# Finished PSUM banks through ScalarE and accumulating transfers instead of VectorE adds: a fused attention and MLP block on one core

## The chip, the cores and the metric

The kernel runs on one core of one Trainium2 chip. The metric is the time of one execution on the device in microseconds; the median of several runs is given. One further execution was profiled, and its trace is what the views quoted here are taken from. The engines are called TensorE (PE), VectorE (DVE), ScalarE (ACT), GpSimd (POOL) and SyncE (SP, which here only issues transfers).

## What is computed

One input `x` of 2048 rows by 576 columns, in float32, is normalised by row. The output is the sum of three things: `x` itself, a sliding local dilated attention of the normalised rows, and a two-layer MLP with a ReLU of the normalised rows.

```python
xn = _layernorm(x, axis=-1)
return x + _A_ref(xn, A_wqkv, A_wo) + _B_ref(xn, B_w1, B_w2)

# _A_ref: 32 heads of 18, each row attends to 8 rows: itself and 2, 4, .. 14 rows before
qkv = x @ wqkv
logits = einsum("bhsd,bhswd->bhsw", q, kg) * scale      # then masked, softmax over the 8
o = einsum("bhsw,bhswd->bhsd", attn, vg)
return o @ wo                                           # 576 x 576
# _B_ref: 576 -> 4608 -> 576
h = maximum(x @ w1, 0)
return h @ w2
```

## The kernel before

**Two phases, row tiles and slots.** The 2048 rows are split in two phases (`ph`) of 1024 rows: the even rows and the odd rows, so that the dilation of two stays within a phase. A phase has eight row tiles of 128 rows (`i`), which the MLP takes in pairs as four row blocks of 256 (`tb`). The 4608 hidden columns are 36 blocks of 128 (`f`), taken three at a time: `C = 3` blocks make a chunk (`c`), and a phase has `NCH = 12` chunks. The list `slots` runs over phase, chunk, row block and hidden block, in this order: 2 x 12 x 4 x 3 = 288 slots. One slot computes one hidden block for one row block (`h_two`, two slots at once and two slots ahead, on the two halves of the rows of TensorE's array) and multiplies an earlier one with its part of `w2` (`o_two`, or `o_mm` in the first seven and the last three slots).

**Precision.** Every operand of a matmul is held as a high and a low part, which a copy on ScalarE (L170, L651) and a subtraction on VectorE (L174, L654) make; each product is three matmuls.

**The output sums.** The three slots of one chunk and row block form a group. They add up in four PSUM banks, `PO[k, h]`: `k` is the row tile of the pair, `h` the half of the columns (`CUT`: 256 and 320). At the last slot of a group (`f == C - 1`) `o_out` empties the four banks: VectorE adds each to the tile `X[ph, i]`, which was loaded with the input rows and so gathers the residual, the MLP and, in chunk `WO_CHUNK = 10`, the output projection of the attention, whose matmuls go to the same banks. In the last chunk the tile is stored by SP one slot later. The next group's matmuls use the same four banks again, after the `h_two` of their first slot.

**Order of the work.** The order on each engine is written out by hand; nothing reorders it. `at(n, ...)` and `late(n, ...)` put a step into slot n, ahead of or behind its `o_two`; `run_splits(n)` at the beginning of a slot splits the weights that are due and has SP load the next staging tile `st`; `run_bg(margin(n))` at the end hands VectorE pieces of the attention as long as its planned time `t["dve"]` stays within `margin` of TensorE's `t["pe"]`. Each `o_out` advances `t["dve"]` for its four adds. Units of attention begin at slot 10 of a phase and every 24 slots after; each has eight slots in which `qkv_tile` adds its matmuls. GpSimd has little to do: memsets for k and v, a mask (`affine_select`), copies of parts of q, and the inverse deviations of the normalisation.

**Buffers.** `xp` has 11 buffers for the tiles `X`: eight of a phase and three more, which `wo_turn` uses for turned tiles of the attention's output before the next phase's rows are loaded into them.

Of the kernel before, what the change touches and what calls it, by code (L numbers as in the profile page):

```python
# [10 lines left out]
F32 = mybir.dt.float32  # L11
F32R = mybir.dt.float32r
AF = mybir.ActivationFunctionType
ALU = mybir.AluOpType
# [4 lines left out]
P = 128  # L19
NPH = 2  # L20
NI = 8
NTB = 4
# [4 lines left out]
C = 3  # L27
# [16 lines left out]
FIRST = 4  # L44
# [14 lines left out]
def tile_body(ctx: ExitStack, tc: tile.TileContext, x, wqkv, wo, w1, w2, out):  # L59
    nc = tc.nc  # L60
    S, D = x.shape
# [4 lines left out]
    NCH = NF // C  # L66
# [3 lines left out]
    CUT = (slice(0, 256), slice(256, D))  # L70
# [6 lines left out]
    pool = lambda name, bufs, **k: ctx.enter_context(tc.tile_pool(name=name, bufs=bufs, **k))  # L77
# [5 lines left out]
        pool(name, 1).tile([P, words], F32, name=name)  # L83

    consts = pool("consts", 1)
    xp = pool("xp", 11)
    xtp = pool("xtp", NTB)
    qop = pool("qop", 1)
    kp = pool("kp", 1)
# [31 lines left out]
    o_v = out.rearrange("(p i two) d -> two i p d", i=NI, two=NPH)  # L121


    t = {"pe": 0.0, "dve": 0.0}
# [16 lines left out]
    def dve(n):  # L141
        t["dve"] += (n + 70) / 960.0
# [113 lines left out]
    X, XT, XN, MR = {}, {}, {}, {}  # L256
# [307 lines left out]
    def run_bg(margin):  # L564

        ran = False
        while bg and t["dve"] + bg[0][0] / 960.0 <= t["pe"] + margin and not (ran and bg[0][0] == 0):
            n, f, a = bg.popleft()
            f(*a)
            if n:  # L570
                ran = True
                dve(n)
# [55 lines left out]
    slots = [(ph, c, tb, f) for ph in range(NPH) for c in range(NCH) for tb in range(NTB) for f in range(C)]  # L628
    H, PO = {}, {}
# [64 lines left out]
    def o_two(n):  # L694


        ph, c, tb, f = slots[n]
        hi, lo = H.pop(n)
        w = W2[ph, c, f]
        with_wo = c == WO_CHUNK and f == C - 1  # L700
        if f == 0:
            o_tiles(n)

        def run(k, h, upper):
            cs, first = slice(k * P, (k + 1) * P), k == upper
            z = [(l[:, cs], w[:, b, W2CUT[h]]) for l, b in ((hi, 0), (hi, 1), (lo, 0))]
            if with_wo:
                more = wo_run(ph, 2 * tb + k, h, (UPPER_MORE if upper else LOWER_MORE) if first else (UPPER if upper else LOWER), upper)
                z = z + more
            return [  # L710
                (PO[k, h], l, r, f == 0 and first and j == 0, f == C - 1 and not first and j == len(z) - 1, CUT[h].stop - CUT[h].start)
                for j, (l, r) in enumerate(z)
            ]

        for j in range(4):
            k, h = divmod(j, 2)
            behind = PB[j - 2] if j > 1 else PB[3] if j == 0 and f else None
            PB[j] = mm_rows((run(k, h, False), run(1 - k, h, True)), behind)
        if with_wo:
            for k in range(2):  # L720
                OT.pop((ph, 2 * tb + k))
        o_out(n, rows=True)
# [3 lines left out]
    def o_mm(n, out=True, which=range(2)):  # L726
        ph, c, tb, f = slots[n]
        hi, lo = H[n]
        w = W2[ph, c, f]
        end = n == len(slots) - 1  # L730
        if f == 0 and 0 in which:
            o_tiles(n)
        for k in which:
            cs = slice(k * P, (k + 1) * P)
            terms = [(j, l, b, h) for j, (l, b) in enumerate(((hi, 0), (hi, 1), (lo, 0))) for h in range(2)]
            if end:
                terms.sort(key=lambda z: -z[3])
            for j, l, b, h in terms:
                mm(
                    PO[k, h], l[:, cs], w[:, b, W2CUT[h]],  # L740
                    f == 0 and j == 0, f == C - 1 and j == 2, D2,
                )
        if 1 in which:
            H.pop(n)
        if out:
            o_out(n, which)

    def store(ph, i):
        nc.sync.dma_start(o_v[ph, i], X[ph, i])

    def o_out(n, which=range(2), rows=False):
        ph, c, tb, f = slots[n]
        if f < C - 1:
            return
        end = n == len(slots) - 1
        t["dve"] = max(t["dve"], t["pe"] - 0.4)
        order = [(k, h) for k in which for h in range(2)]
        if rows:
            order.sort(key=lambda z: z[1])
        elif end:  # L760
            order.sort(key=lambda z: (z[0], -z[1]))
        for k, h in order:
            i = 2 * tb + k
            acc, cols = X[ph, i], CUT[h]
            nc.vector.tensor_tensor(acc[:, cols], PO[k, h], acc[:, cols], op=ALU.add)  # L765
            dve(cols.stop - cols.start)
            if end and k:
                (nc.scalar if h else nc.sync).dma_start(o_v[ph, i][:, cols], acc[:, cols])
            elif end and h == 0:
                store(ph, i)  # L770
            elif c == NCH - 1 and h == 1 and not end:
                at(n + 1, store, ph, i)


    todo = {}

    def at(n, f, *a):
        todo.setdefault(n, []).append((f, a))
# [3 lines left out]
    def late(n, f, *a):  # L782
        todo_late.setdefault(n, []).append((f, a))
# [61 lines left out]
    both, x_low, w_low, last = TERMS[0:4], TERMS[4:8], TERMS[9:13], [TERMS[8], TERMS[13]]  # L845
# [61 lines left out]
    h4[0]()  # L907
    h4[1]()
    o_out(2, (0,))
    x4 = make_xt(0, 4, parts=True)  # L910
    for f in x4[:3]:
# [11 lines left out]
        (late if k else at)(z, {"stats": stats, "norm": norm, "xt": make_xt}[op], 0, *a)  # L923
    for tb in range(NTB):
        late((8, 8, 9, 7)[tb], twin, tb)
    def margin(n):

        odd, qkv = n % 2 == 0, n + 1 in qkv_slots
        if n + 1 in busy_m | bounded and not qkv:
            return 1.4  # L930
        due = sum(z[0] <= n + 1 for z in (*staged, *tasks))
        if slots[n][3] == 1:
            return (1.8 if odd else 2.7 + 2.4 * qkv) - 0.8 * due + 1.6 * (odd and qkv)
        return (2.5 if odd else 3.5 + 2.4 * qkv) - 0.8 * due + 1.6 * (odd and qkv)
# [6 lines left out]
    for n in range(FIRST, len(slots)):  # L941
        if n == ROW0:
            AHEAD["n"] = 4
        run_splits(n)
        g = n - n % 2 + LAG
        if n < ROW0:
            h_mm(n + LAG)
        elif g < len(slots):
            h_two(g, n % 2 == 1)
        for f, a in todo.pop(n, []):  # L950
            f(*a)
        if ROW0 - 1 <= n < len(slots) - C:
            o_two(n)
        else:
            o_mm(n)
        for f, a in todo_late.pop(n, []):
            f(*a)
        run_bg(margin(n))
# [27 lines left out]
```

## Time and profile before

| | |
|---|---|
| median of 3 runs | 1143.41 us (1143.14 to 1143.69) |
| span of the profiled execution, first to last instruction | 1141.6 us |
| TensorE busy | 1134.5 us, 99% |
| VectorE busy | 802.1 us, 70% |
| ScalarE busy | 303.0 us, 27% |
| GpSimd busy | 57.1 us, 5% |
| moved by the DMA engines | 83.6 MB, 73 GB/s |

The profile gives no other time for the profiled execution than its span; the median of the runs is 1.8 us above it. The page has the busy time of each engine, the span in 40 slices, the DMA queues, the chain of work that ended last, groups of instructions by line with what they waited for, and DMA issues. A line such as L765 is a line of the kernel; where a helper issues the instruction it is the helper's line. Busy time on TensorE is modelled from the ends of pipelined matmuls.

### The profile page before, as it was taken

What the parts mean: (1) busy time and instruction counts of PE and PEld (TensorE: products, weight loads), DVE (VectorE), ACT (ScalarE), POOL (GpSimd) and SP (SyncE); (2) the same over time, 40 slices, a digit from 0 to 9 for tenths busy, and PEclk for the clock granted to TensorE, in tenths of its full rate; (3) what the DMA queues carried; (4) which work ended last, traced back from release to release, by engine and by line L of the source; (5) the groups of instructions that cost most, each with busy time, mean ns of one, the idle gap of its engine ahead of it and who ended that gap; (6) DMA issues with size and microseconds to landing.
All of it is one profiled execution on the core that took longest, in us unless ns stands there. A gap on an engine that the chain in (4) does not pass through costs nothing.

```text
span 1141.6 us, 38695 instructions
## 1 busy us (share of the span) xinstructions
PE 1134.5 (99%) x17224; PEld 1128.4 (99%) x17224; DVE 802.1 (70%) x1522; ACT 303.0 (27%) x854; POOL 57.1 (5%) x84
## 2 busy tenths in 40 slices
PE   8999999999999999999999999999999999999998
PEld 8999999999999999999999999999999999999998
DVE  7415886887788689854674179868868887896433
ACT  4412222222232212322462122222222312222110
POOL 2400000000000000000110000000000000010000
PEclk9999999999999999999999999999999999999999
DMA  6303212130330312622633033032221304136002
GB/s 192 109 2 94 71 47 67 48 98 6 97 98 13 104 33 50 175 57 63 157 122 98 2 101 88 23 85 63 63 59 47 107 2 114 45 81 152 13 2 84
DMA packets 118855, 83.60 MB, mean 73 GB/s; under 512 B 33201, under 2 KB 102449, under 8 KB 118689
## 3 DMA queue, kind: packets, MB, share of 16 engines
q1 hardware_dynamic: 118256, 80.67, 25.6%
q8 instruction: 135, 2.21, 0.8%
q10 hardware_dynamic: 432, 0.46, 0.1%
q14 instruction: 32, 0.25, 0.1%
HBM read 64.95 MB, written 7.96 MB: 64 GB/s over the span
## 4 chain that ended last, share of the span: by engine, by line
PE 96%; issue 2%; DVE 1%; ACT 0%; DMA 0%; DVEq 0%; POOL 0%; ACTq 0%
PE po L137 41%; PE pm L137 28%; PE ph L137 24%; PE ph L127 1%; PE po L127 1%; PE pm L317 0%; DVE pr L544 0%; DMA x<-in_x 0%; PE pm L369 0%; DVE xn L613 0%; PE pm L127 0%; DVE hlo L654 0%; DVE x L765 0%; ACT xT L322 0%; DVE xn L614 0%
## 5 line engine op out<-in xcount | busy, mean ns | idle before, releaser
L137 PE MATMUL po<-w2t,hhi 64*128 64x256 f32 (+1 forms) x4448 | 444.8, 290 | 0.0
L137 PEld LDWEIGHTS po<-w2t,hhi 64*128 64x128 f32 x4448 | 356.1, 184 | 0.6
L137 PE MATMUL po<-w2t,hlo 64*128 64x256 f32 (+1 forms) x2224 | 331.2, 287 | 0.0
L137 PE MATMUL ph<-xT,w1t 64*128 64x256 f32 x4806 | 305.5, 273 | 0.3 <-DVE hlo L654 0.2
L137 PEld LDWEIGHTS ph<-xT,w1t 64*128 64x128 f32 x4806 | 293.7, 184 | 1.5 <-DVE hlo L654 1.1
L765 DVE TENSOR_TENSOR x<-po,x 128x320 f32<-128x320 f32 (+1 forms) x384 | 149.6, 449 | 149.4 <-PE po L137 146.8
L137 PEld LDWEIGHTS po<-w2t,hlo 64*128 64x128 f32 x2224 | 217.2, 184 | 0.0
L651 ACT ACTIVATE hhi<-ph 128x256 fp32r<-128x256 f32 x187 | 62.1, 382 | 496.8 <-PE ph L137 484.6
L137 PE MATMUL pm<-wq,xT 64*128 64x432 f32 x1728 | 178.8, 354 | 0.0
L137 PE MATMUL pm<-xT,w1t 64*128 64x256 f32 x2700 | 170.6, 273 | 0.0
L137 PEld LDWEIGHTS pm<-xT,w1t 64*128 64x128 f32 x2700 | 164.5, 184 | 0.0
L137 PEld LDWEIGHTS pm<-wq,xT 64*128 64x128 f32 x1728 | 160.0, 184 | 2.9
L654 DVE SCALAR_TENSOR_TENSOR hlo<-ph,hhi 128x256 fp32r<-128x256 f32 x187 | 70.8, 418 | 129.6 <-ACT hhi L651 129.5
L651 ACT ACTIVATE hhi<-pm 128x256 fp32r<-128x256 f32 x101 | 33.3, 381 | 214.1 <-PE pm L137 214.1
L505 DVE TENSOR_TENSOR pr<-qo,k 128x1152 f32<-128x1152 f32 x64 | 85.6, 1348 | 0.0
L508 DVE TENSOR_REDUCE lg<-pr 128x64 f32<-128x1152 f32 x64 | 85.3, 1342 | 0.0
L537 DVE TENSOR_TENSOR pr<-lg,v 128x1152 f32<-128x1152 f32 x64 | 85.0, 1348 | 0.3
L544 DVE TENSOR_TENSOR pr<-pr 128x288 f32<-128x288 f32 (+1 forms) x128 | 70.1, 600 | 0.1
L654 DVE SCALAR_TENSOR_TENSOR hlo<-pm,hhi 128x256 fp32r<-128x256 f32 x101 | 38.2, 418 | 32.9 <-ACT hhi L651 32.1
L170 ACT ACTIVATE w2t<-st 128x256 fp32r<-128x256 f32 (+1 forms) x144 | 56.3, 445 | 7.1 <-PE po L137 3.9
L174 DVE TENSOR_TENSOR w2t<-st,w2t 128x256 fp32r<-128x256 f32 (+1 forms) x142 | 57.9, 448 | 0.1
L174 DVE TENSOR_TENSOR w1t<-st,w1t 128x640 fp32r<-128x640 f32 x68 | 55.6, 817 | 2.4 <-ACT w1t L170 2.2
(99 smaller groups left out, 689.8 us busy)
## 6 DMA issues: line engine op xcount, KB each, us to landing
st<-in_w SPq DMA_DIRECT2D x72, 288.0 KB, 3.3
st<-in_w SPq DMA_DIRECT2D x72, 256.0 KB, 3.1
st<-in_wqkv SPq DMA_DIRECT2D x32, 216.0 KB, 3.0
st<-in_w SPq DMA_DIRECT2D x144, 32.0 KB, 2.8
out<-x SPq DMA_DIRECT2D x15, 288.0 KB, 2.4
x<-in_x SPq DMA_DIRECT2D x14, 288.0 KB, 4.4
k<-k SPq DMA_DIRECT2D x8, 441.0 KB, 3.9
v<-v SPq DMA_DIRECT2D x8, 441.0 KB, 4.7
```

What stands on the lines that cost most here:

```text
L127: nc.tensor.matmul(o, l, r, start=start, stop=stop)
L137: ins = nc.tensor.matmul(o, l[z], r[z], start=start, stop=stop)
L170: nc.scalar.activation(hi, src, AF.Copy)
L174: nc.vector.tensor_tensor(lo, src, f32(hi), op=ALU.subtract)
L505: nc.vector.tensor_tensor(pr[i], q, window(k, i), op=ALU.mult)
L508: nc.vector.tensor_reduce(lg[:, i], pr.pop(i).rearrange(heads, d=Dh), axis=AX.X, op=ALU.add)
L537: nc.vector.tensor_tensor(pr[i].rearrange(heads, d=Dh), e, window(v, i).rearrange(heads, d=Dh), op=ALU.mult)
L544: nc.vector.tensor_tensor(o, z[:, 0:n], z[:, n : 2 * n], op=ALU.add)
L651: nc.scalar.activation(hi, pt, AF.Relu)
L654: nc.vector.scalar_tensor_tensor(lo, pt, 0.0, f32(hi), op0=ALU.max, op1=ALU.subtract)
L765: nc.vector.tensor_tensor(acc[:, cols], PO[k, h], acc[:, cols], op=ALU.add)
```

## The change

The output sums are no longer kept in the chip's memory through the phase. Chunk 0 of a phase still adds the banks to `X` on VectorE, but writes the result to a staging tile `ev`, which SP stores to the output. In each later chunk ScalarE copies the four banks to two staging tiles, and when both halves of a tile are there, GpSimd issues a transfer that adds the tile to the output in memory (`accum_op`). The pool `evp` has three staging tiles, which take the room of the three buffers by which `xp` becomes smaller. The very last group is handled in another way: `last_sums`, in slot 285, has SP load the two output tiles back to staging tiles, VectorE adds the last banks to them, and they are stored. There are 174 accumulating transfers of 128 x 576 words (288 KB). The planned time of VectorE no longer counts the adds that are gone.

```diff
-    xp = pool("xp", 11)
+    xp = pool("xp", 8)
+    evp = pool("evp", 3)
...
-    def store(ph, i):
-        nc.sync.dma_start(o_v[ph, i], X[ph, i])
-
     def o_out(n, which=range(2), rows=False):
...
         end = n == len(slots) - 1
-        t["dve"] = max(t["dve"], t["pe"] - 0.4)
+        last = ph == NPH - 1 and c == NCH - 1 and tb == NTB - 1
+        if c == 0 or last:
+            t["dve"] = max(t["dve"], t["pe"] - 0.4)
...
         for k, h in order:
             i = 2 * tb + k
-            acc, cols = X[ph, i], CUT[h]
-            nc.vector.tensor_tensor(acc[:, cols], PO[k, h], acc[:, cols], op=ALU.add)
-            dve(cols.stop - cols.start)
-            if end and k:
-                (nc.scalar if h else nc.sync).dma_start(o_v[ph, i][:, cols], acc[:, cols])
-            elif end and h == 0:
-                store(ph, i)
-            elif c == NCH - 1 and h == 1 and not end:
-                at(n + 1, store, ph, i)
+            cols = CUT[h]
+            if last:
+                acc = EV[k]
+                nc.vector.tensor_tensor(acc[:, cols], PO[k, h], acc[:, cols], op=ALU.add)
+                dve(cols.stop - cols.start)
+                if k:
+                    (nc.scalar if h else nc.sync).dma_start(o_v[ph, i][:, cols], acc[:, cols])
+                elif h == 0:
+                    nc.sync.dma_start(o_v[ph, i], acc)
+                continue
+            if k not in EV:
+                EV[k] = evp.tile([P, D], F32, name="ev")
+                EVN[k] = 0
+            acc = EV[k]
+            if c == 0:
+                nc.vector.tensor_tensor(acc[:, cols], PO[k, h], X[ph, i][:, cols], op=ALU.add)
+                dve(cols.stop - cols.start)
+            else:
+                nc.scalar.activation(acc[:, cols], PO[k, h], AF.Copy)
+            EVN[k] += 1
+            if EVN[k] == 2:
+                del EV[k]
+                if c == 0:
+                    at(max(n + 1, FIRST), nc.sync.dma_start, o_v[ph, i], acc)
+                else:
+                    nc.gpsimd.dma_start(o_v[ph, i], acc, accum_op=ALU.add)
+
+    EV, EVN = {}, {}
+
+    def last_sums():
+
+        for k in range(2):
+            EV[k] = evp.tile([P, D], F32, name="ev")
+            nc.sync.dma_start(EV[k], o_v[NPH - 1, NI - 2 + k])
...
+    late(len(slots) - C, last_sums)
```

## The prediction

> **What bounds the kernel now.** I read the page first: busy shares, the slices, the shares of the chain.
>
> ```profile
> span 1141.6 us, 38695 instructions
> ...
> PE 1134.5 (99%) x17224; PEld 1128.4 (99%) x17224; DVE 802.1 (70%) x1522; ACT 303.0 (27%) x854; POOL 57.1 (5%) x84
> ...
> q1 hardware_dynamic: 118256, 80.67, 25.6%
> ...
> PE 96%; issue 2%; DVE 1%; ACT 0%; DMA 0%; DVEq 0%; POOL 0%; ACTq 0%
> ```
>
> TensorE is busy for 99% of the span and carries 96% of the chain that ended last. The change takes nothing from TensorE, so the next question is where TensorE stands still. The windows before, inside and after the steady part say it (after the length: busy time and count of PE, PEld, DVE, ACT and POOL, the granted clock, the DMA share, GB/s).
>
> ```profile
> 0.00:10.00 10.00, 6.99 (x44) 6.19 (x45) 4.88 (x13) 5.94 (x11) 4.41 (x12) 1.00 0.75 212
> 10.00:1131.00 1121.00, 1120.67 (x17117) 1115.68 (x17117) 793.29 (x1499) 296.41 (x842) 52.69 (x73) 1.00 0.26 72
> 1131.00:1142.00 11.00, 6.87 (x70) 6.54 (x66) 3.91 (x10) 0.66 (x2) 0.00 (x0) 0.95 0.29 107
> ```
>
> The view of waits says who held whom up (total, times, longest):
>
> ```profile
> DVE x L765 <- PE po L137: 146.8, 75, 8.4
> ...
> PEld ph L137 <- DVE hlo L654: 1.1, 3, 0.4
> ```
>
> In the 1121 us of the middle window TensorE runs at the full clock and is idle for 1121.00 - 1120.67 = 0.33 us. VectorE holds its weight loads up for 1.1 us in all, and VectorE's adds (L765) spend 146.8 us waiting for TensorE, not the other way. Everything else that could be saved lies in the first 10 us and the last 11. So relieving VectorE can give at most about 1 us, and the question is what the new path costs: in the steady part, at the start and at the end.
>
> **What leaves VectorE and lands on ScalarE.** Rows for the adds, and for ScalarE reading a PSUM bank of each width:
>
> ```profile
> L765 DVE TENSOR_TENSOR x<-po,x 128x320 f32<-128x320 f32 x192 | 84.5, 480 | 15.2 <-PE po L137 12.6 <-PE po L127 2.6
> ...
> L765 DVE TENSOR_TENSOR x<-po,x 128x256 f32<-128x256 f32 x192 | 72.7, 419 | 134.2 <-PE po L137 134.2
> ...
> L651 ACT ACTIVATE hhi<-ph 128x256 fp32r<-128x256 f32 x187 | 62.1, 382 | 496.8 <-PE ph L137 484.6 <-PE ph L127 12.2
> ...
> L612 ACT ACTIVATE k<-pm 128x320 fp32r<-128x320 f32 x16 | 6.2, 444 | 23.8 <-issue 23.8
> ```
>
> There are 384 adds. Those of chunk 0 stay (2 phases x 8 row tiles x 2 halves = 32), and so do the last four; 348 go, 174 of each width: 174 x (0.480 + 0.419) = 156 us off VectorE, most of it time in which it would otherwise have waited. ScalarE gets 174 x (0.382 + 0.444) = 144 us and goes from 303 to 447 us, 39% of the span.
>
> Does a busier ScalarE delay TensorE? It is in order, so the copies of a finished group stand ahead of the next slot's weight splits (L170) and, in every second group, of the next two relus (L651). A group's four copies take 0.66 us for the narrow pair and about 0.85 for the wide one, and end about 1.3 us after the first starts; the four adds took 1.55 us from the same start. TensorE comes back to those banks only after the next slot's `h_two`, 1.6 us later. The relus have 484.6 us of waiting before them, and their results are used more than a slot later. I cost this at nothing; the cover is ScalarE's idle time, and without it the price would be the 1 us or so by which a split can push a relu, in a few dozen slots.
>
> **The staging tiles.** `evp` has three buffers and each group takes two. So the second tile of a group waits for the transfer of the first tile of the group before. The spacing of groups between the qkv steps is in the times of the adds:
>
> ```profile
> 102.67 1.55 DVE L765 TENSOR_TENSOR x<-po,x 128x256 f32<-128x256 f32 x4 [1.07 <-PE po L137]
> ...
> 111.88 1.55 DVE L765 TENSOR_TENSOR x<-po,x 128x256 f32<-128x256 f32 x4
> ...
> 121.21 1.55 DVE L765 TENSOR_TENSOR x<-po,x 128x256 f32<-128x256 f32 x4 [0.57 <-PE po L137]
> ```
>
> It is (121.21 - 102.67) / 2 = 9.3 us. From the start of a second tile's first copy to the end of the first tile's second copy, where its transfer may be issued, lie about 0.8 us (0.38 + 0.44). So a transfer that takes less than L = 9.3 - 0.8 = 8.5 us from issue to landing costs nothing here. Queued behind such a wait would be ScalarE's other copies, then its splits and relus, and TensorE waits for those.
>
> **How long is L?** The trace shows no GpSimd transfer and no accumulation; it is bounded by rows of DMA issues (the last number is us to landing; the line of landings is that of the stores to the output) and of GpSimd's own work:
>
> ```profile
> out<-x SPq DMA_DIRECT2D x15, 288.0 KB, 2.4
> x<-in_x SPq DMA_DIRECT2D x14, 288.0 KB, 4.4
> ...
> st<-in_wo SPq DMA_DIRECT2D x8, 288.0 KB, 2.8
> ```
>
> ```profile
> DMA to landing us min/median/max: 2.1/2.4/4.7
> ```
>
> ```profile
> L546 POOL COPY qo<-qo 128x64 f32<-128x64 f32 x16 | 9.6, 623 | 152.1 <-DVE qo L544 152.1
> ...
> L172 POOL TENSOR_TENSOR w1t<-st,w1t 128x640 fp32r<-128x640 f32 x4 | 6.2, 1562 | 1.1 <-ACT w1t L170 1.1
> ```
>
> From below, an accumulation is no quicker than the plain store of the same tile, 2.4 us. From above, it is the slowest store (4.7), after the load of a tile in the crowded start (4.4), after an issue as long as GpSimd's longest operation here less SP's own 0.35 (1.2): 10.3 us. I take a quiet load and a store in series, since the sum has to be read before it is written, and 0.6 us (the COPY row) for GpSimd's issue: 2.8 + 2.4 + 0.6 = 5.8 us, an estimate. That is under 8.5. So nothing is lost in the steady part. 174 transfers of 0.295 MB add 51 MB to q1's 81 MB, and as much again if the destination is read through the same engines: the DMA share goes from 26% to some 42 to 58%, with no queue full. On GpSimd, 174 x 0.4 to 1.6 us beside 57 us is still under a third of the span. The affine select and the copies of q that wait there for VectorE stand ahead of a transfer for a few us at most, since `margin` plans VectorE no more than 3.5 + 2.4 us ahead.
>
> **The start.** In chunk 0 the adds stay on VectorE and write to staging, and SP stores each tile: 16 stores that replace those at the ends of the phases. SP now waits for an add before it issues the loads queued behind it. The rows are of the timeline of SP, of VectorE and of ScalarE:
>
> ```profile
> 15.60 0.39 SPq L182 DMA_DIRECT2D st<-in_w  x1
> ...
> 33.15 0.38 SPq L182 DMA_DIRECT2D st<-in_w  x1
> ```
>
> ```profile
> 25.62 0.81 DVE L765 TENSOR_TENSOR x<-po,x 128x256 f32<-128x256 f32 x2
> ...
> 34.71 1.55 DVE L765 TENSOR_TENSOR x<-po,x 128x256 f32<-128x256 f32 x4
> ```
>
> ```profile
> 37.75 0.73 ACT L170 ACTIVATE w1t<-st 128x640 fp32r<-128x640 f32 x1
> ...
> 41.24 0.72 ACT L170 ACTIVATE w1t<-st 128x640 fp32r<-128x640 f32 x1
> ```
>
> The load issued at 15.60 moves behind the stores of the first two tiles, whose adds end at 26.43: it lands near 31, and its split was at 37.75. The load of 33.15 moves behind adds that end at 36.26, and lands near 41, just as its split starts (41.24); TensorE uses that weight chunk only from slot 10. Nothing is lost; without that cover it would be the lateness of one load, 1 to 2 us. The store of tile 0 lands near 28, and the add that needs its buffer comes at 35.5.
>
> **The end.** Here I find the price. The last group's four banks are added on VectorE to sums that SP has to load back from the output first. The second load (`ev` for k=1) takes the buffer of the first tile of the group three slots before, so SP must wait for that tile's transfer to land, and only then read.
>
> ```profile
> 1131.12 1.55 DVE L765 TENSOR_TENSOR x<-po,x 128x256 f32<-128x256 f32 x4 [3.10 <-PE po L137]
> ...
> 1136.78 1.60 DVE L765 TENSOR_TENSOR x<-po,x 128x320 f32<-128x320 f32 x4 [2.58 <-PE po L127]
> ...
> 1137.22 0.30 PE L127 MATMUL po<-w2t,hlo 128*128 128x320 f32 x1
> ```
>
> The copies begin where the adds did, 1131.12. The first tile is complete after 0.66 + 0.44 us, at 1132.2. The transfer lands at 1132.2 + 5.8 = 1138.0, and the load, 2.8 us, at 1140.8. The add for k=1 was ready to start when its bank was, 1137.22 + 0.30 = 1137.5. So the end moves by 1140.8 - 1137.5 = 3.3 us; the last adds and the store follow as before. The first load (k=0) waits for the transfer of a group 9.3 us earlier, and is there in time.
>
> The sum: 0 in the steady part, 0 at the start, +3.3 at the end: a span of 1141.6 + 3.3 = 1144.9 us. The median of the runs, 1143.41, lies 1.8 us above the span; the page has no other time for the profiled execution, so I carry that over: **1146.7 us**. A change of 0.2% is 2.3 us, about what a measurement of this kernel can tell from none.
>
> **Rivals.** *Not slower: the sum is loaded back almost in time.* The mechanism is a short L: the end moves by L + 2.8 + 1132.2 - 1137.5 = L - 2.5, so at the plain store's 2.4 us it moves by nothing, and it stays under 2.3 us up to L = 4.8. For it: stores near the end took 2.1 us, and the DMA engines are quiet there. Against it: the destination has to be read, for which the shortest row is 2.8. Its middle, L = 3.6, gives 1143.4 + 1.1 = 1144.5 us. [...] I give this rival 0.32.
>
> *The staging buffers become the bound.* If L is over 8.5 us, each group between qkv steps is lengthened by L - 8.5. By the code some 56 of the 96 groups are so close (24 have qkv steps, 8 the output projection, 8 are chunk 0), in about 11 runs, each of which absorbs about 1.1 us first. At the upper bound L = 10.3: 56 x 1.8 - 11 x 1.1 = 89 us, and 7.8 at the end: near 1240 us. For it: L is unknown and the transfers share engines with the weight loads. Against it: it needs an accumulation about three times as long as a store. 0.11.
>
> *Faster.* It would take more than TensorE's idle time in the steady part, 0.33 us, and none of the three mechanisms above. 0.02.
>
> **How the numbers follow.** The forecast (L from 4.8 to 8.5, 1145.7 to 1149.4) has 0.55, not slower 0.32, the staging bound 0.11, faster 0.02. The range leaves the staging bound out and takes in the rest, with 1 us above for small stalls: 1143.2 to 1150.5. Faster by over 0.2%: 0.03, since a rest must be left for what I do not see; within 0.2%: 0.32; slower: 0.65.
>
> **What would show it.** Right: TensorE idle in the steady part still under 2 us; ScalarE near 447 us and VectorE near 646; transfers from GpSimd landing in 5 to 7 us; in the last 11 us the add for k=1 waiting some 3 us for the load of `ev`, and that load waiting on SP for the transfer. Wrong: copies on ScalarE waiting for transfers and TensorE waiting for PSUM (staging), or no wait at the end (a short L), or TensorE waiting for relus that stand behind copies.

## The result, and the profile after

The changed kernel takes **1160.44 us** (median of 4 runs, 1160.24 to 1163.68) against 1143.29 us for the kernel before on the same chip (4 runs, 1143.14 to 1143.69): a ratio of 1.0158, 95% interval 1.0143 to 1.0172. It is slower by 17 us, where 3.3 us were forecast; the upper end of the range was 1150.5. The profiled execution has a span of 1158.5 us, 16.9 above the one before.

From the page of the changed kernel: busy shares, the queue of GpSimd's transfers (packets, MB, share of 16 engines' span), the group of the issues on GpSimd, and the DMA issue with its median time to landing.

```profile
span 1158.5 us, 39105 instructions
...
PE 1140.7 (98%) x17224; PEld 1131.2 (98%) x17224; DVE 671.3 (58%) x1174; ACT 415.2 (36%) x1202; POOL 211.4 (18%) x258
...
q0 software_dynamic: 25056, 51.33, 31.4%
q1 hardware_dynamic: 118832, 81.85, 24.9%
...
L789 POOL DMA_DIRECT2D out<-ev x174 | 153.3, 1033 | 857.7 <-ACT ev L782 831.9
...
out<-ev POOLq DMA_DIRECT2D x174, 288.0 KB, 5.7
```

The steady part between start and end, in the view of windows of the changed kernel (length; busy time of PE, PEld, DVE, ACT and POOL; granted clock; DMA share; GB/s):

```profile
0.00:10.00 10.00, 8.01 (x43) 7.11 (x44) 4.79 (x13) 6.03 (x11) 4.31 (x12) 1.00 0.76 216
10.00:1148.00 1138.00, 1128.80 (x17156) 1120.41 (x17155) 664.65 (x1158) 409.19 (x1192) 206.94 (x247) 1.00 0.57 116
1148.00:1159.00 11.00, 3.88 (x30) 3.68 (x28) 1.85 (x5) 0.00 (x0) 0.16 (x1) 0.90 0.56 131
```

TensorE's idle time in the middle is now 1138.00 - 1128.80 = 9.2 us, where it was 0.33. Who held TensorE up (total, times, longest), still of the changed kernel:

```profile
PE po L138 <- ACT k L599: 8.0, 2, 4.6
...
PE ph L138 <- DVE hlo L655: 0.7, 1, 0.7
```

So 8.0 of the 9.2 us are two waits, one in each phase, at the same place: the first product of the output projection (it begins at slot 122 of a phase, in chunk `WO_CHUNK`), whose operand, the high part of the turned attention output, is written by ScalarE at L599 (L598 before). Why ScalarE was late is in its timeline (start, length, instruction, idle time before it and what ended that), first of the changed kernel, then of the kernel before:

```profile
484.56 0.74 ACT L599 ACTIVATE k<-xn 128x640 fp32r<-128x640 f32 x1 [6.75 <-DMA xn<-words]
```

```profile
479.54 0.74 ACT L598 ACTIVATE k<-xn 128x640 fp32r<-128x640 f32 x1 [1.70 <-DMA xn<-words]
```

ScalarE stood idle for 6.75 us: it was not busy with copies, it waited for a load. That load of turned attention output (`wo_turn` stores the output to `words` in memory and loads it back turned) is 5.0 us late.

TensorE issues the same 17,224 matmuls in the same order in both traces, so the n-th of one can be set against the n-th of the other. Up to slot 122 of the first phase the changed kernel is 0.0 us behind. There it falls 4.6 us behind by the wait and another 2.8 us in the 8 us that follow, 7.4 in all. The windows of the changed kernel show why the second part comes:

```profile
480.50:485.35 4.85, 0.21 (x5) 0.01 (x3) 0.02 (x1) 0.74 (x1) 0.00 (x0) 0.90 0.78 174
485.35:488.50 3.15, 3.15 (x29) 3.15 (x31) 0.96 (x2) 0.00 (x0) 0.00 (x0) 0.50 0.70 196
488.50:492.50 4.00, 4.00 (x42) 4.00 (x42) 0.00 (x0) 0.00 (x0) 0.00 (x0) 0.66 0.52 83
492.50:496.00 3.50, 3.50 (x58) 3.50 (x58) 0.00 (x0) 0.66 (x2) 0.00 (x0) 1.00 0.00 0
```

The 0.66 is the mean of a window in which the clock changes: in narrower windows it is 0.50 from 484.4 to 491.1 and 1.00 from 491.2 on. So around the 4.6 us without work TensorE is granted half its clock for 6.8 us, of which it works through 5.8. 0.50 x 5.8 = 2.9 us of full-speed work are missing, and the lag grew by 2.8. After the stop in the second phase, of 3.4 us, the granted clock is 0.50 for 3.4 us, from 1057.8 to 1061.2, and 1.00 behind that.

The rest of the path: 0.7 us is regained, 2.0 lost at the boundary of the phases (turned rows loaded late), 0.2 regained, 6.0 lost at slot 122 of the second phase (a wait of 3.4 and the clock after it), 0.5 regained: TensorE ends 14.0 us late. The last 2.8 us come behind it, in the timelines of VectorE and of SP at the end of the changed kernel:

```profile
1150.78 0.82 DVE L767 TENSOR_TENSOR ev<-po,ev 128x320 f32<-128x320 f32 x2 [2.58 <-PE po L128]
1154.84 0.82 DVE L767 TENSOR_TENSOR ev<-po,ev 128x320 f32<-128x320 f32 x2 [3.24 <-DMA ev<-out]
```

```profile
1143.64 7.59 SPq L797 DMA_DIRECT2D ev<-out  x2
```

The add for k=1 waits 3.24 us for the sum that SP loads back, and SP needs 7.59 us for the two issues because the second waits for a transfer. This is the prediction's step for the end.

**Why the loads are late.** The share of the 16 DMA engines in three windows: the 25 us before slot 122 of the first phase, the phase boundary, and the 30 us around slot 122 of the second phase. First the kernel before, then the changed one.

```profile
455.00:480.00 25.00, 25.00 (x417) 25.00 (x416) 22.36 (x45) 8.92 (x21) 1.63 (x2) 1.00 0.73 179
545.00:578.00 33.00, 32.81 (x545) 32.55 (x541) 23.19 (x60) 18.68 (x44) 3.64 (x8) 1.00 0.73 193
1020.00:1050.00 30.00, 30.00 (x496) 30.00 (x494) 23.72 (x49) 9.08 (x21) 2.08 (x4) 1.00 0.69 168
```

```profile
455.00:480.00 25.00, 25.00 (x418) 25.00 (x416) 14.16 (x27) 12.74 (x31) 5.10 (x6) 1.00 0.99 195
545.00:578.00 33.00, 32.95 (x539) 32.69 (x536) 12.94 (x33) 18.92 (x44) 10.54 (x16) 1.00 0.78 146
1020.00:1050.00 30.00, 29.97 (x494) 29.77 (x494) 16.20 (x34) 14.66 (x37) 5.71 (x8) 1.00 0.94 184
```

The kernel before used 26% of the DMA engines on average and 73% here. From the line of queue q0, one accumulating transfer holds 31.4% x 16 x 1158.5 / 174 = 33.5 engine-us, which is 2.1 us of all 16 engines. Six are issued in the first window (the x6 of POOL): 6 x 2.1 / 25 = 0.50; measured in this window, GpSimd's queue takes 0.52, and SP's falls from 0.72 to 0.47. By this sum, an estimate, the demand is 1.23 of what there is: a backlog of 0.23 x 25 = 5.8 us, where the load came 5.0 us late. SP shows the same backlog in its timeline from 465 on, first before, then changed:

```profile
465.99 2.59 SPq L377 DMA_DIRECT2D words<-x  x4
...
473.57 0.38 SPq L405 DMA_DIRECT2D xn<-words  x1
```

```profile
465.98 4.16 SPq L378 DMA_DIRECT2D words<-x  x4
...
477.63 0.43 SPq L406 DMA_DIRECT2D xn<-words  x1
```

Both begin with the four stores to `words` at the same time; the changed kernel needs 4.16 us to issue them instead of 2.59, longer for the weight loads behind them too, and reaches the load that TensorE will wait for 4.1 us later. From there to ScalarE's start it is 6.9 us instead of 6.0, which makes up the 5.0.

### The profile page after: what moved, and what is told of

Read it like the earlier page. It is cut to its first block, busy times and chain, and to the rows that moved or that the text cites. A ratio compares the mean times of both kernels' runs of the same rounds, so it can differ in the third digit from the quotient of the medians.

```text
span 1158.5 us, 39105 instructions
## 1 busy us (share of the span) xinstructions
PE 1140.7 (98%) x17224; PEld 1131.2 (98%) x17224; DVE 671.3 (58%) x1174; ACT 415.2 (36%) x1202; POOL 211.4 (18%) x258
## 3 DMA queue, kind: packets, MB, share of 16 engines
q0 software_dynamic: 25056, 51.33, 31.4%
HBM read 65.54 MB, written 59.87 MB: 108 GB/s over the span
## 4 chain that ended last, share of the span: by engine, by line
PE 85%; issue 10%; DMA 2%; DVE 2%; POOL 1%; ACT 0%; SPq 0%; DVEq 0%; POOLq 0%; ACTq 0%
PE po L138 35%; PE pm L138 26%; PE ph L138 21%; POOL out L789 1%; PE ph L128 1%; PE po L128 1%; DMA xn<-words 0%; DMA xT<-words 0%; DVE pr L538 0%; DVE pr L545 0%; DMA out<-ev 0%; DMA ev<-out 0%; PE pm L318 0%; DMA x<-in_x 0%; PE pm L370 0%
## 5 line engine op out<-in xcount | busy, mean ns | idle before, releaser
L138 PEld LDWEIGHTS po<-w2t,hhi 64*128 64x128 f32 x4448 | 352.2, 184 | 0.9
L138 PE MATMUL po<-w2t,hlo 64*128 64x256 f32 (+1 forms) x2224 | 327.2, 287 | 0.0
L789 POOL DMA_DIRECT2D out<-ev x174 | 153.3, 1033 | 857.7 <-ACT ev L782 831.9
L655 DVE SCALAR_TENSOR_TENSOR hlo<-ph,hhi 128x256 fp32r<-128x256 f32 x187 | 71.1, 420 | 263.3 <-ACT hhi L652 262.2
L138 PEld LDWEIGHTS po<-w2t,hlo 64*128 64x128 f32 x2224 | 213.2, 185 | 0.2 <-DVE hlo L655 0.2
L782 ACT ACTIVATE ev<-po 128x256 f32<-128x256 f32 (+1 forms) x348 | 115.9, 415 | 220.9 <-PE po L138 220.3
L138 PEld LDWEIGHTS pm<-wq,xT 64*128 64x128 f32 x1728 | 157.6, 184 | 5.1
L652 ACT ACTIVATE hhi<-pm 128x256 fp32r<-128x256 f32 x101 | 33.5, 386 | 113.9 <-PE pm L138 113.9
L655 DVE SCALAR_TENSOR_TENSOR hlo<-pm,hhi 128x256 fp32r<-128x256 f32 x101 | 38.1, 418 | 43.2 <-ACT hhi L652 43.2
```

Source lines behind the costliest of these rows:

```text
L138: ins = nc.tensor.matmul(o, l[z], r[z], start=start, stop=stop)
L652: nc.scalar.activation(hi, pt, AF.Relu)
L655: nc.vector.scalar_tensor_tensor(lo, pt, 0.0, f32(hi), op0=ALU.max, op1=ALU.subtract)
L782: nc.scalar.activation(acc[:, cols], PO[k, h], AF.Copy)
L789: nc.gpsimd.dma_start(o_v[ph, i], acc, accum_op=ALU.add)
```

## The experiments

The theory (A): nothing but the time for which the accumulating transfers hold the DMA engines makes the kernel slow, at the places where these were nearly full already; the loads there come late, and TensorE's clock adds to it. The rivals: ScalarE's copies (B), the place of the waiting loads in the order of the work (C), and the accumulating as such rather than the share (A2). In the expectations below the letters are each run's own. All ratios are against runs of the kernel before on the same chip.

**Without the eight transfers ahead of slot 122.**

```diff
-                else:
+                elif n % SPP not in (116, 119):
                     nc.gpsimd.dma_start(o_v[ph, i], acc, accum_op=ALU.add)
```

> The changed kernel without 8 of its 174 accumulating transfers: those of the groups that end in slots 116 and 119 of each phase, the two groups just ahead of the output projection's first group; their sums are missing from the output. Theory A (the transfers slow the round trip of the turned attention tiles through memory, the words out and back, on the DMA engines they share, and TensorE then waits for the split of those tiles and is granted a lower clock after it): the two stalls at slot 122 of each phase go, TensorE's lag behind the kernel before no longer jumps by 7.3 and 5.8 us there, and the time falls from 1160.4 to about 1148 (1146 to 1151). Rival B (the stall comes from the new order of work on ScalarE, VectorE or SP, not from traffic): no change, 1159 to 1161.

Measured 1149.96 us (10 runs, 1146.77 to 1154.15), ratio 1.0053 (1.0034 to 1.0073). The stall at the output projection is gone in both phases, and 10.5 of the 17 us with it, for 8 of 174 transfers. TensorE ends 3.2 us late, and all of that arises at the phase boundary, where the DMA share now shows as 0.91. So the cost isn't spread: it sits in the windows where the engines' share is highest.

**Plain stores instead of accumulating ones.**

```diff
-                    nc.gpsimd.dma_start(o_v[ph, i], acc, accum_op=ALU.add)
+                    nc.gpsimd.dma_start(o_v[ph, i], acc)
```

> The changed kernel with every accumulating transfer turned into a plain store from GpSimd of the same tile to the same place; the output then holds only each tile's last partial sum. Theory A1 (bytes and packets of any kind crowd the engines): the destination is no longer read, so issue to landing falls from 5.7 to 3 to 4 us, and the stalls shrink to about half: 1150 to 1155. Theory A2 (it is the accumulating that occupies the engines): stalls almost gone, end earlier by 2, about 1145 to 1148. Rival B (order of work, or GpSimd's issuing as such): 1157 to 1160.

Measured 1145.36 us (10 runs, 1143.84 to 1153.99), ratio 1.002 (1.0001 to 1.0039). This is in the range of its theory A2, by which the accumulating occupies the engines, and under that of A1, by which bytes and packets of any kind crowd them. From its page and the first of its windows:

```profile
q0 software_dynamic: 13920, 51.33, 12.9%
...
out<-ev POOLq DMA_DIRECT2D x174, 288.0 KB, 3.0
```

```profile
455.00:480.00 25.00, 25.00 (x418) 25.00 (x416) 13.97 (x27) 12.59 (x32) 3.21 (x6) 1.00 0.81 231
```

The same bytes in the same 174 transfers hold the engines for 12.9% x 16 x 1143.8 / 174 = 13.6 engine-us, 0.85 us of all 16, and land in 3.0 us; accumulating costs 2.5 times that, and 144 packets a tile instead of 80. Demand in the window is 0.73 + 6 x 0.85 / 25 = 0.93, under 1, by the same estimate; the row shows 0.81, since SP moved less in the window than before: 231 GB/s less some 71 for the six stores are 160, an estimate, against 179. ScalarE's copies, the staging tiles and the issues on GpSimd are all still there. What is left is 1.7 us against the kernel before (1143.66 on this chip), most of it a wait of 1.1 us at the first slot 122.

**The kernel before with the traffic added.** VectorE goes on adding; 16 stores of chunk 0 and 174 accumulating transfers of the tiles `x` to spare memory are put in.

```diff
             nc.vector.tensor_tensor(acc[:, cols], PO[k, h], acc[:, cols], op=ALU.add)
+            if h == 1 and c == 0:
+                at(max(n + 1, FIRST), nc.sync.dma_start, beside[ph * NI + i], acc)
+            elif h == 1 and not (ph == NPH - 1 and c == NCH - 1 and tb == NTB - 1):
+                nc.gpsimd.dma_start(beside[ph * NI + i], acc, accum_op=ALU.add)
```

> The kernel before, with VectorE's adds and its own stores as they are, and beside them the same 16 stores and 174 accumulating transfers of the x tiles from GpSimd to a piece of memory of their own that nobody reads. No ScalarE copies, no staging tiles, no load at the end. Theory A (traffic alone): stalls at slot 122 of both phases and at the phase boundary as in the changed kernel, 1143.3 plus 10 to 14, so 1153 to 1158. Rival B (ScalarE's copies, the staging tiles or the new order on VectorE): 1143 to 1145.

Measured 1167.35 us (4 runs, 1165.92 to 1173.11), ratio 1.021 (1.0174 to 1.0246). The waits of TensorE:

```profile
PE po L138 <- ACT k L599: 7.0, 2, 3.7
PE ph L138 <- ACT xT L415: 5.5, 1, 5.5
```

The traffic alone, with no copy on ScalarE and no staging tile, makes the same stalls at the same places. It is slower than the expected range, and the trace shows where: 5.5 us at the phase boundary. There this kernel also stores its tiles still; that this is the reason was not tested.

**The copies on VectorE instead of ScalarE.**

```diff
-        if c == 0 or last:
+        if True:
...
-                nc.scalar.activation(acc[:, cols], PO[k, h], AF.Copy)
+                nc.vector.tensor_copy(acc[:, cols], PO[k, h])
+                dve(cols.stop - cols.start)
```

> The changed kernel with the copies of finished banks to the staging tiles on VectorE instead of ScalarE, planned there as the adds were; transfers as they were. Theory A (traffic): ScalarE's 144 us of copies cost nothing, so the stalls stay at the same three places and the time within 3 us of the changed kernel, 1157 to 1164. Rival B (copies that stand ahead of splits in ScalarE's queue make the stalls): 1145 to 1150.

Measured 1165.99 us (4 runs, 1163.13 to 1167.98), ratio 1.0195 (1.0176 to 1.0214). TensorE waits 7.0 us in two places for the same L599. Rival B falls: ScalarE is back at 303 us of work and the stalls are where they were. The time is 2 us above the expected range, with a longer wait at the phase boundary (3.3 us).

**The turned loads earlier.** For the first three tiles, steps of `wo_turn` (stores to `words`, loads back) are moved ahead by three slots.

```diff
-TURN_STEPS = ((-10, -9, -7, -4), (-7, -5, -3, -1), (-4, -3, 0, 1), (-2, 0, 1, 2))
+TURN_STEPS = ((-13, -12, -10, -7), (-10, -8, -6, -1), (-7, -6, 0, 1), (-2, 0, 1, 2))
```

> The changed kernel, all of it, with the turn and the sending of the first three turned attention tiles three slots earlier, and the fetching back of tile 0 three and of tile 1 three slots earlier (the split of tile 1 and what follows stay where they were). Theory A (the round trip is lengthened by the accumulating transfers, and its slack was used up): the two stalls at slot 122 go or shrink to under 2 us in all, with the spell of lower clock behind them: 1160.4 less 11 to 13 us, 1147 to 1150, with L and the traffic as they were. Rival B (the stall is tied to the order on ScalarE or VectorE at that slot): 1158 to 1161. Rival C (the transfers keep the queue so full that an earlier start is only an earlier wait): 1153 to 1157.

Measured 1154.95 us (4 runs, 1153.21 to 1156.76), ratio 1.0107 (1.0092 to 1.0122): 5.5 us better, and not cured. This is the range of the expectation's last rival, by which an earlier start is only an earlier wait. ScalarE's waits and TensorE's, from the view of waits:

```profile
ACT w2t L171 <- DMA st<-in_w: 12.0, 2, 6.6
```

```profile
PE po L138 <- ACT ev L782: 3.5, 2, 1.9
```

The wait of 6.75 us for the turned words has become a wait of 6.6 us for a staged weight chunk, with the copies of a finished group queued behind it on ScalarE, and TensorE waiting for those. The backlog was handed to another load. It costs less there: TensorE stops for 1.9 us in the first phase and 1.6 in the second, and its clock is 1.00 in the windows from 472 to 493 and from 1020 to 1050.

**The last sums loaded earlier, first attempt.** Meant: `last_sums` three slots earlier and into free buffers of `xp`.

```diff
-            EV[k] = evp.tile([P, D], F32, name="ev")
+            EV[k] = xp.tile([P, D], F32, name="x")
...
-    late(len(slots) - C, last_sums)
+    late(len(slots) - 2 * C, last_sums)
```

> The changed kernel with the last group's two sums loaded back into free buffers of the pool of x tiles, three slots earlier, so that no load waits for a transfer of the group before. Theory (the end pays for the wait on the staging buffer): the add for k=1 waits no more for the load, the end comes about 2.9 us earlier, 1157.5 (1157 to 1158). Rival (another wait stands behind it, such as the load itself or the stores): less than 1 us, 1159.5 to 1160.5.

Measured 1159.91 us (4 runs, 1156.85 to 1166.64), ratio 1.0152 (1.0104 to 1.02). In this kernel the copies of the group before go to these tiles as well, and 2 of the 174 transfers are left out by that. The span is 1156.2; the last four adds run in a row, and what follows TensorE's end is about as long as before the change (-0.2 us instead of +2.8), but TensorE itself ended 14.7 us late instead of 14.0. The medians of 4 runs, which spread over 10 us, don't show the gain.

**Both together.** The steps of `wo_turn` as above, and the last sums in tiles of their own (`LAST`), in slot 282.

```diff
-                acc = EV[k]
+                acc = LAST[k]
...
-            EV[k] = evp.tile([P, D], F32, name="ev")
-            nc.sync.dma_start(EV[k], o_v[NPH - 1, NI - 2 + k])
+            LAST[k] = xp.tile([P, D], F32, name="x")
+            nc.sync.dma_start(LAST[k], o_v[NPH - 1, NI - 2 + k])
```

> The same, and the last group's sums loaded into two free buffers of the pool of x tiles three slots earlier, kept apart from the staging tiles. Theory (the end's price is the wait of the second load for a staging buffer): 2.9 us less than the kernel with the earlier turn alone, 1144 to 1147, and no wait of the add for k=1. Rival: less than 1 us.

Measured 1152.29 us (4 runs, 1148.85 to 1156.74), ratio 1.0086 (1.0059 to 1.0112): 2.7 us less than with the earlier turn alone, as the theory says, but far above its range, which took the earlier turn to cure the stalls; and the runs of the two kernels overlap. The profiled execution was the longest of the four; in it TensorE loses 5 us between 604 and 1037 us in small amounts, with a clock shown as 1.00 and no wait to match, for which I have no cause.

**And the loads at the phase boundary moved too.**

```diff
-    (-6, -1, 0, 1, 2, 4, 6), (-5, 0, 2, 3, 4, 7, 8), (-3, 2, 4, 5, 6, 8, 9), (4, 6, 7, 10),
+    (-6, -1, 0, 0, 1, 3, 6), (-5, 0, 2, 2, 3, 5, 8), (-3, 2, 4, 4, 5, 7, 9), (4, 6, 7, 10),
```

> As the kernel with earlier turns and the earlier last load, and in addition the turn, the sending and the fetching back of the first three tiles of the second phase's input one slot earlier. Theory A: the remaining stall at the phase boundary (1.9 us in the changed kernel) goes too, and the time is that of the kernel before within 0.3%: 1142.5 to 1146. Rival: TensorE has lost something that is spread over all slots, which would leave 1148 or more.

Measured 1156.95 us (4 runs, 1149.89 to 1158.55), ratio 1.0112 (1.0081 to 1.0144). Far above the expected range: TensorE still waits 3.2 us at the boundary, by the view of waits for the low part of a hidden block (L655 on VectorE), and at the output projection as in the two runs above. With those runs this bears on rival C: in the three orders tried, order decided which load was late, and how dear that was, not whether one was. That no other order would do better is not shown.

**Two and three plain stores of each tile.** Is it the time that the engines are held, or the reading and adding in memory? Each tile is stored plainly to the output and once (or twice) more to spare memory.

```diff
-                    nc.gpsimd.dma_start(o_v[ph, i], acc, accum_op=ALU.add)
+                    nc.gpsimd.dma_start(o_v[ph, i], acc)
+                    for z in range(1):          # 2 in the run with three stores
+                        nc.gpsimd.dma_start(beside[(z * NPH + ph) * NI + i], acc)
```

> The changed kernel with its 174 transfers as plain stores from GpSimd, and each tile stored a second time into spare memory (348 stores; the sums are left out, so only the last partial of each tile stands in the output). It asks whether the stalls come from the share of the DMA engines' time that the transfers take, or from the accumulating as such. Theory A (share): a plain store of a tile held the 16 engines for 0.85 us (12.9% of 1143.8 us by 174), an accumulating one for 2.1 us. In the 25 us before slot 122 the kernel before uses 0.73 of the engines; six groups with two plain stores each add 0.41, in all 1.14, a backlog of about 3.5 us at the output projection in each phase, less than the changed kernel's. Time 1148 to 1155 us, DMA share of the window 455 to 480 at 0.95 or more, and a wait of 1 to 4 us of the first product of the output projection. Rival (accumulating as such, that is the reading of memory and adding): no stall however many plain stores, 1144 to 1147 us as with one store.

> As the run with two plain stores, with each tile stored three times (522 stores, sums left out). Theory A: three stores hold the engines for 2.55 us, a fifth more than an accumulating transfer's 2.1, so demand in the window 455 to 480 is 0.73 + 0.61 = 1.34 and the stalls are at least those of the changed kernel: 1158 to 1175 us. Rival (accumulating as such): 1144 to 1150 us. Either way GpSimd's issue, 3 x 0.54 = 1.6 us in a turn of 3.9, still fits.

Measured with two stores 1156.98 us (4 runs, 1155.72 to 1159.23), ratio 1.0119 (1.0102 to 1.0136); with three 1173.39 us (1169.87 to 1174.25), ratio 1.0254 (1.0238 to 1.0271). The kernel with two stores, from its page, its windows and its waits:

```profile
q0 software_dynamic: 27840, 102.65, 25.0%
```

```profile
455.00:480.00 25.00, 25.00 (x418) 25.00 (x416) 13.98 (x27) 12.68 (x32) 6.40 (x12) 1.00 0.92 281
```

```profile
PE po L139 <- ACT k L600: 7.4, 2, 3.8
```

One plain store makes no such stall (1.1 us in the first phase), two make the one of the accumulating kernel, in its place (stops of 3.6 and 3.8 us, then 2.7 and 3.0 us more; the granted clock averages 0.994 over the execution, 0.995 in the accumulating kernel). Nothing is accumulated here, so A2 falls. The waits lie in the expected range; the time is 2 us above its own, in which no term stood for the clock, and the window's share, 0.92, is below the 0.95 expected. So the sum of demand says which kernel stalls, and not exactly how full the engines show. With three stores, inside the expected range, the queue takes 36.5% of the engines. TensorE then waits 9.3 us for the same split of turned words, 4.5 us at the phase boundary, and 2.0 us for ScalarE's copies, which stand behind splits of weights that were loaded late. Set in order of the share that GpSimd's queue takes, the five kernels are one row: 0% 1143.4 us, 12.9% 1145.4, 25.0% 1157.0, 31.4% (accumulating) 1160.4, 36.5% 1173.4. The kernel before with the traffic added (31.0%, 1167.4) and the one with copies on VectorE (31.2%, 1166.0) lie above this row, with longer waits at the boundary. All of this traffic leaves through GpSimd's queue; no run sends it through another, so the engines' time is not parted from something that belongs to this queue.

**Without 14 transfers, and then with the end mended.** Left out are those ahead of slot 122 in both phases and three groups ahead of the phase boundary. The second run adds `LAST` as above.

```diff
-                else:
+                elif n % SPP not in (116, 119) and n not in (134, 137, 140):
                     nc.gpsimd.dma_start(o_v[ph, i], acc, accum_op=ALU.add)
```

> The changed kernel without the transfers of 14 of its 174 groups: those ending in slots 116 and 119 of both phases (ahead of the output projection), and in slots 134, 137 and 140 of the first phase (ahead of the phase boundary); their sums are missing. Theory A: with the transfers gone from the two places where the engines are full, all three stalls go and only the last load's 2.9 us at the end is left: 1145 to 1148 us, and an end of TensorE's work within 1 us of the kernel before. Rival (the 160 transfers that are left cost something everywhere, or the stalls move to the groups next to those left out): 1149 us or more.

> The run without those 14 transfers, and in addition the last two sums are loaded back three slots earlier, into two free buffers of the pool of x instead of staging tiles, so that no load waits for the transfer of the group before. It closes the sum: what the changed kernel lost beside the three stalls should be the wait at the end. Theory A with the prediction's step (e): the 2.9 us at the end go, TensorE's end stays within 2 us of the kernel before, and the time is 1143.5 to 1146 us, by which ScalarE's 348 copies and 160 transfers cost nothing that a measurement can tell. Rival (the end is set by something else, or the 160 transfers slow the chip a little everywhere): 1147 us or more.

Measured 1147.56 us (5 runs, 1146.89 to 1148.39), ratio 1.0034 (1.0021 to 1.0047), and 1144.75 us (11 runs, 1143.61 to 1150.29), ratio 1.002 (1.0007 to 1.0034). TensorE ends 1.2 and 0.7 us late (in the first of the two a wait of 1.2 us at the output projection is left); the last adds of the second run wait for no load (its timeline of VectorE):

```profile
1137.46 1.60 DVE L767 TENSOR_TENSOR x<-po,x 128x320 f32<-128x320 f32 x4 [2.58 <-PE po L128]
```

That closes the sum, in medians: 1160.4 to 1150.0 by the output projection's two places, to 1147.6 by the phase boundary, to 1144.8 by the end. The step at the boundary is not clear of the spread of the runs without eight transfers (1146.77 to 1154.15); their trace shows the wait there, 1.9 us, and the trace without 14 no longer does. 160 accumulating transfers, all copies and all staging tiles are left, and some 1 us of cost. No kernel of this study is faster than the kernel before; the fastest that still forms all sums is the one with both moves, at 1152.29 us.

## Why the prediction was wrong, and where it was right

**The step that failed** is the last of the part on the staging tiles: "the DMA share goes from 26% to some 42 to 58%, with no queue full". The number came out (0.57 in the steady part); the conclusion didn't. An average over the span was set against full, where the loads that TensorE waits for are issued in windows that were at 0.73 and 0.69 already; with the transfers these show 0.99 and 0.94, and the loads come up to 5.0 us late. The profile before had it: the window ahead of the output projection shows a share of 0.73 at 179 GB/s. Six tiles in 25 us are 71 GB/s, or 142 if the destination is read through the same engines, as the prediction allowed: at the same rate that is 0.29 to 0.58 more, at or over 1 from end to end. The term "0 in the steady part" measured 14.0 us: 8.0 in two waits, 2.0 at the boundary, and the rest in the main at half clock, for which the sum had no term at all. The sign of being right that failed is TensorE's idle time in the steady part, 9.2 us against under 2; none of the three signs of being wrong that the prediction gave is what came.

**The duration of one transfer was right and was used for the wrong question.** L was taken as 5.8 us and measured 5.7 (median; 3.9 to 10.0). No run shows that it is made up as the prediction made it up, a load and a store in series and 0.6 us of issue (the issue measured 0.94), so the close agreement may be luck. It was weighed only as the time for which a staging tile is held. The other half of a transfer's price is how long it holds the engines that others need, 2.1 us of all 16. The same bytes hold them 33.5 / 13.6 = 2.5 times as long as in a plain store; how much of this is the read of the destination, the adding or the smaller packets, no run parts. In the profile's count of memory read the destination does not show (64.95 MB before, 65.54 after; the 0.59 more are the two tiles loaded back at the end).

**The staging tiles cost nothing, as forecast**: ScalarE's copies wait for a transfer for 0.6 us in all. **ScalarE costs nothing, as forecast**; the sizes were off, 415 us instead of 447 and 671 on VectorE instead of 646, since means of overlapping instructions were multiplied where busy times add up (the 348 copies of 415 ns on average are busy for 115.9 us, not 144). **The start cost nothing**: at slot 122 TensorE was 0.0 us behind. **The end** was forecast at 3.3 us and is 2.8, by the mechanism forecast, the wait itself 3.24; taking it away gave 1147.56 - 1144.75 = 2.8.

**The rivals.** Not slower by a short L: L was not short. From GpSimd a plain store landed in 3.0 us (the run with plain stores) and the accumulating transfer in 5.7, nearly twice as long. The staging bound: not seen, not even with three stores, where ScalarE's copies wait for a transfer for 0.6 us again. That the transfers "share engines with the weight loads" stood there as a remark in favour of the staging bound; it should have been a rival of its own, with loads of the attention as its place.

## What to carry to other kernels

Traffic that is added to a kernel like this one is weighed in the window that is fullest, against the loads that the bounding engine waits for there, and not against the mean share of the span; price it by the time for which it holds the engines, not only by the time that it takes to land. An accumulating transfer counted here as two and a half stores of the same bytes (33.5 engine-us against 13.6). The changed kernel's stops of 4.6 and 3.4 us cost TensorE 7.4 and 6.0 us in all, most of the difference by the half clock, where a stop of 1.9 us at the output projection left the clock at 1.00 in the kernel with earlier turns; so if a load must be late, let it be one that leaves TensorE work in hand.

## What was not expected of the hardware

An accumulating transfer of 288 KB: 5.7 us to landing against 3.0, 144 packets against 80, 0.94 us of issue on GpSimd (median) against 0.54. While the engines were nearly full (0.99 in the window from 455 to 480), SP's own issues became slower, 4.16 us for four stores that had taken 2.59. TensorE's granted clock around a stop: 0.50 for 6.8 us with a stop of 4.6 us, and for 3.4 us with one of 3.4. The length of the stop alone doesn't decide it: the clock averaged 1.00 over the execution with plain stores, which has a stop of 1.1 us, and was 1.00 from 472 to 493 us around the 1.9 us of the one with earlier turns, but in the run without eight transfers it averaged 0.91 from 566 to 586 us, around a stop of 1.9 us at the boundary.
